# A DiT block on one core: program order made by a list scheduler, x and the FFN weights resident, attention interleaved with the FFN

## The chip, the cores and the metric

The kernel runs on one core of one Trainium2 chip. Time is device time in microseconds (us), from the first to the last instruction of the program. The kernel makes an instruction list for each of five engines, and they run side by side: TensorE (matmuls; PE in the profile, its weight loads PEld), VectorE (DVE), ScalarE (ACT), GpSimd (POOL) and SyncE (SP, which issues the transfers here). The kernel orders them against one another with semaphores.

Every kernel was run several times, and the text gives the median of its runs. Each comparison uses runs of the same chip and the same rounds. A run that is over 1.5 % above the fastest of its kernel counts as slow and is left out of the ratios. A *profiled span* is the span of the one execution that was traced; it is 0.4 to 3.2 us shorter than the median time, and I say which of the two a number is.

## The reference, cut to what matters

```python
# S = 2048 tokens, D = 512, H = 32 heads of 16, F = 1792, everything bf16
mod = (silu(c) @ w_mod)                        # six vectors of 512: sa, ca, ga, sb, cb, gb
h = layernorm(x) * (1 + ca) + sa
q, k, v = h @ wqkv                             # 512 x 1536
# token s sees only the 8 tokens s, s-2, ..., s-14 (window 8, dilation 2)
attn = softmax(q . k[s - 2w] / 4  over w)      # masked where s - 2w < 0
x = x + ga * ((attn . v[s - 2w]) @ wo)
h = layernorm(x) * (1 + cb) + sb
x = x + gb * ((silu(h @ w1) * (h @ w3)) @ w2)  # 512 x 1792, twice, and 1792 x 512
```

Both kernels work on 16 tiles T of 128 tokens and 4 chunks of 512. The attention, with a window of only 8 tokens, makes no matmul of Q with K. Instead VectorE multiplies Q with eight shifted copies of K (the *QK product*, 128x4096 elements), TensorE sums the product over each head with a 0/1 matrix, softmax follows, VectorE multiplies eight shifted copies of V with the weights (the *AV product*), and TensorE sums over the eight shifts with identity matmuls. V goes to DRAM and comes back shifted by a strided load.

Of the kernel before, what the change touches and what calls it, by code (L numbers as in the profile page):

```python
# [1 line left out]

# [8 lines left out]
P = 128  # L11
# [8 lines left out]
NDT = D // P  # L20
NFT = F // P
# [3 lines left out]
XN_SLOTS = 8  # L25
VT_SLOTS = 8
NSL = 6
POOL_BANKS = (0, 1, 4, 5)
OY_BANKS = (2, 3)
L_BANKS = (6, 7)  # L30


class _Sem:
    __slots__ = ("h", "count", "producer")

    def __init__(self, h):
        self.h = h
        self.count = 0
        self.producer = None


class KernelBuilder:
    ENGS = ("sp", "pe", "dve", "act", "pool")

    def __init__(self, nc, ctx: ExitStack):
        self.nc = nc
        self.ctx = ctx
        self.streams = {e: [] for e in self.ENGS}
        self.sems = {}
        self.waited = {}  # L50

    def sem(self, name) -> _Sem:
        s = self.sems.get(name)
        if s is None:
            h = self.ctx.enter_context(self.nc.semaphore(name))
            s = _Sem(h)
            self.sems[name] = s
        return s

    def _inc(self, eng, name, n):  # L60
        s = self.sem(name)
        if s.producer is None:
            s.producer = eng
        assert s.producer == eng, f"sem {name} incremented by {eng} and {s.producer}"
        s.count += n
        return s

    def cur(self, name):
        return self.sem(name).count

    def wait(self, eng, name, value):
        if value is None or value <= 0:
            return
        s = self.sem(name)
        assert value <= s.count, f"wait on {name} for {value} but only {s.count} scheduled (deadlock)"
        key = (eng, name)
        if self.waited.get(key, 0) >= value:
            return
        self.waited[key] = value
        h = s.h  # L80
        self.streams[eng].append(lambda e, h=h, v=value: e.wait_ge(h, v))

    def emit(self, eng, fn, inc=None, incn=1):
        if inc is not None:
            s = self._inc(eng, inc, incn)
            h = s.h
            self.streams[eng].append(lambda e, fn=fn, h=h, n=incn: fn(e).then_inc(h, n))
            return s.count
        self.streams[eng].append(lambda e, fn=fn: fn(e))
        return None  # L90

    def dma(self, eng, out_ap, in_ap, inc):
        s = self._inc(eng, inc, 16)
        h = s.h
        nc = self.nc

        def fn(e, out_ap=out_ap, in_ap=in_ap, h=h):
            with nc.allow_non_contiguous_dma(reason="layout dma"):
                e.dma_start(out_ap, in_ap).then_inc(h, 16)

        self.streams[eng].append(fn)
        return s.count

    def replay(self):
        nc = self.nc
        with nc.Block() as block:
            for eng in self.ENGS:
                fns = self.streams[eng]
                if not fns:
                    continue  # L110
                starter = {"sp": block.sync, "pe": block.tensor, "dve": block.vector,
                           "act": block.scalar, "pool": block.gpsimd}[eng]

                def section(e, fns=fns):
                    for fn in fns:
                        fn(e)

                starter(section)
# [6 lines left out]
def bass_adaLN_cond__sliding_local_dilated__glu_gated_swiglu__prompt_kernel(  # L125
    nc, A_x, A_wqkv, A_wo, B_x, B_w1, B_w3, B_w2, c, w_mod, out, dbg=None
):
    ctx = ExitStack()
    with ctx:
        kb = KernelBuilder(nc, ctx)  # L130
        _build(kb, A_x, A_wqkv, A_wo, B_w1, B_w3, B_w2, c, w_mod, out)
        kb.replay()


def _build(kb: KernelBuilder, A_x, A_wqkv, A_wo, B_w1, B_w3, B_w2, c, w_mod, out):
    nc = kb.nc
    ctx = kb.ctx
    sp, pe, dve, act, pool = "sp", "pe", "dve", "act", "pool"
    bf = dt.bfloat16
    f32 = dt.float32  # L140
# [4 lines left out]
    A_x = _full_ap(A_x)  # L145
    A_wqkv = _full_ap(A_wqkv)
    A_wo = _full_ap(A_wo)
    B_w1 = _full_ap(B_w1)
    B_w3 = _full_ap(B_w3)
    B_w2 = _full_ap(B_w2)  # L150
    c = _full_ap(c)
    w_mod = _full_ap(w_mod)
    out = _full_ap(out)
    x2d = A_x.flatten_outer_dims()
    out2d = out.flatten_outer_dims()
    x_view = x2d.rearrange("(t p) d -> p t d", p=P)

    x_res = [sb([P, D], bf, f"x_res{i}") for i in range(2)]
    x1_tok = sb([P, NT, D], bf, "x1_tok")
    hT = sb([P, NDT, 2, 512], bf, "hT")  # L160
    regW = sb([P, NDT, 3 * D], bf, "regW")
    wqkv_sb = regW
    wo_sb = sb([P, NDT, D], bf, "wo_sb")
    NWS = 6
    w13 = [sb([P, NDT, 2 * P], bf, f"w13_{i}") for i in range(NWS)]
    w2_sb = sb([P, NFT, D], bf, "w2_sb")
    hhb = [sb([P, NFT, 512], bf, f"hh{i}") for i in range(2)]
    hh = hhb[0]
    xn = sb([P, XN_SLOTS, D], bf, "xn")
    stats = [sb([P, NT, 6], f32, f"stats{i}") for i in range(2)]  # L170
    mv = [sb([P, NT, 2], f32, f"mv{i}") for i in range(2)]
    rsn = [sb([P, NT, 2], f32, f"rsn{i}") for i in range(2)]
    cst = sb([P, 4], f32, "cst")
# [3 lines left out]
    ident = sb([P, P], bf, "ident")  # L177
    E_sb = sb([P, NDT, H], bf, "E_sb")
    ones_bf = sb([P, P], bf, "ones_bf")
    cT = sb([P, NDT], bf, "cT")  # L180
    thc = sb([P, NDT], f32, "thc")
    csT = sb([P, NDT], f32, "csT")
    csT_bf = sb([P, NDT], bf, "csT_bf")
# [3 lines left out]
    attn = [sb([P, W, H], bf, f"attn{i}") for i in range(2)]  # L187
    Eexp = [sb([P, W, H], f32, f"Eexp{i}") for i in range(2)]
    oT_sb = [sb([P, NDT, P], bf, f"oT{i}") for i in range(2)]
    o_sb = [sb([P, D], bf, f"osb{i}") for i in range(2)]  # L190
    ga_bc = sb([P, D], bf, "ga_bc")
    gb_bc = sb([P, D], bf, "gb_bc")
    csb = sb([P, NDT, P], bf, "csb")
    junk = [sb([P, D], bf, f"junk{i}") for i in range(2)]

    wbase = nc.lookup_mloc(regW).addr

    def wsb(shape, dtype, name, off):
        return nc.alloc_sbuf_tensor_at("sb_" + name, shape, dtype, offset=wbase + off)

    thb = [wsb([P, 512], bf, f"thb{i}", 3072 * i) for i in range(4)]
    gbf = [wsb([P, 512], bf, f"gbf{i}", 3072 * i + 1024) for i in range(4)]
    ubf = [wsb([P, 512], bf, f"ubf{i}", 3072 * i + 2048) for i in range(4)]

    ARENA = 90112
    arena = sb([P, ARENA], dt.uint8, "arena")
    abase = nc.lookup_mloc(arena).addr

    def asb(shape, dtype, name, off):
        return nc.alloc_sbuf_tensor_at("sb_" + name, shape, dtype, offset=abase + off)  # L210

    qT = asb([P, NDT, S], bf, "qT", 0)
    kT = asb([P, NDT, S], bf, "kT", 16384)
    prodQK = [asb([P, W, NDT, P], bf, f"prodQK{i}", 32768 + 8192 * i) for i in range(2)]
    x_ln = asb([P, NT, D], bf, "x_ln", 73728)
    v_tok = asb([P, VT_SLOTS, D], bf, "v_tok", 49152)
    for i in range(4, NSL):
        thb.append(asb([P, 512], bf, f"thb{i}", 49152 + 3072 * (i - 4)))
        gbf.append(asb([P, 512], bf, f"gbf{i}", 49152 + 3072 * (i - 4) + 1024))
        ubf.append(asb([P, 512], bf, f"ubf{i}", 49152 + 3072 * (i - 4) + 2048))  # L220
    vsh = [asb([P, W, D], bf, f"vsh{i}", 57344 + 8192 * i) for i in range(2)]
    prodAV = [asb([P, W, D], bf, f"prodAV{i}", 73728 + 8192 * i) for i in range(2)]
    wmA = asb([P, NDT, 1536], bf, "wmA", 57344)


    hh_base = nc.lookup_mloc(hh).addr
    wmB = nc.alloc_sbuf_tensor_at("sb_wmB", [P, NDT, 1536], bf, offset=hh_base)

    v_dram = nc.dram_tensor("v_scratch_dram", (S, D), bf)

    PALL = ctx.enter_context(nc.psum_tensor("pall", [P, 8 * 512], f32))

    def bank_f32(b):
        return PALL[:, b * 512:(b + 1) * 512]

    def bank_bf16(b):
        return PALL[:, b * 512:(b + 1) * 512].bitcast(bf)

    pool_state = {"next": 0, "release": {}}

    def pool_acquire():
        i = pool_state["next"]
        pool_state["next"] += 1
        nb = len(POOL_BANKS)
        if i >= nb:
            eng_, semname, val = pool_state["release"][i - nb]
            kb.wait(pe, semname, val)
# [703 lines left out]
```

## The kernel before: what the change and the argument touch

The program order is written by hand. `do_step(s)` starts the QK product of tile s, the softmax of tile s-1, the AV product of s-2, the sums of s-3, the residual of s-4 and LayerNorm 2 behind that:

```python
    def do_step(s, allow_ffn=True):
        if in_range(s - 1):
            L_vals[s - 1] = qk_reduce(s - 1)
            smx_vals[s - 1] = softmax_max(s - 1)
        if in_range(s - 3):
            O_vals[s - 3] = av_acc(s - 3)
        # ... (softmax, QK product of s, AV product of s-2, shifted V load, residual, LN2) ...
                if g == 0:      # after LN2 of chunk 0: ONE VectorE instruction scales all of w2
                    scal["w2"] = kb.emit(dve, lambda e: e.scalar_tensor_tensor(w2_sb[:], w2_sb[:], 0.5, bass.AP(gb_bc, ...),
                                                                              op0=ALU.mult, op1=ALU.mult), inc="dve_p")
                enqueue_ffn_chunk(g)
        if allow_ffn:
            emit_ffn_units(UNITS_PER_STEP, W2_PER_STEP)     # 3.5 FFN units and one w2 product per step
    # ... QKV of all four chunks is issued among do_step(0) ... do_step(10), with allow_ffn=False ...
    do_step(10, allow_ffn=False)
    for s in range(11, nsteps):
        do_step(s)                                          # FFN units only from here
```

No FFN unit can start before QKV of all chunks is done, because the FFN's scratch tiles lie in the memory of `wqkv`. The FFN weights are streamed, each column group once per chunk, so four times:

```python
    def w13_load(n):                                  # n = 14 * chunk + fi
        # ... wait for the slot n % 6 ...
        kb.dma(sp, w13[s_][:, :, 0:P], w1_view[:, :, fi * P:(fi + 1) * P], inc=...)
        w13_dma_val[n] = kb.dma(sp, w13[s_][:, :, P:2 * P], w3_view[:, :, fi * P:(fi + 1) * P], inc=...)
```

ScalarE normalises for LayerNorm, sums for LayerNorm 2 (two passes with an accumulator) and copies both FFN results out of PSUM. x is loaded a second time, tile by tile, for the residual.

## Time and profile before

| Kernel before | |
|---|---|
| time, median of 4 runs | 312.89 us (312.24 to 318.33) |
| profiled span | 311.0 us |
| TensorE's work at full clock | 254 us |
| TensorE's lost time (span less that work) | 57 us |
| first QKV / first QK product / first AV product / first FFN matmul | 21.4 / 31.9 / 53.3 / 120.4 us |
| moved by DMA | 47.2 MB |

The second part of the profile's page gives the busy tenths of each engine in 40 equal slices of 7.8 us; PEclk is TensorE's granted clock in tenths. These are the lines of TensorE, VectorE and the clock, then the engine shares of the chain of work that ended last, of the kernel before:

```profile
PE   0557971899999978399779999989999999999996
DVE  3790655968998999978993999642546435455521
PEclk9999997699999999779979999999999999999999
...
PE 64%; DVE 19%; ACT 6%; POOL 4%; issue 4%; DMA 2%; SPq 0%; DVEq 0%; ACTq 0%
```

TensorE is full from two thirds of the span on, and has holes in the first half. The windows view gives each engine's busy us and instruction count in a stretch, then the granted clock, the DMA engines' busy share and the rate in GB/s. Kernel before:

```profile
core 0: us, PE busy (x) PEld busy (x) DVE busy (x) ACT busy (x) POOL busy (x), PEclk, DMA share, GB/s
0.00:20.00 20.00, 5.47 (x56) 3.34 (x57) 12.53 (x37) 10.33 (x14) 14.66 (x49) 1.00 0.84 289
20.00:40.00 20.00, 17.79 (x125) 9.14 (x125) 10.03 (x29) 16.34 (x27) 9.71 (x33) 1.00 0.60 205
40.00:60.00 20.00, 10.24 (x117) 7.01 (x116) 12.63 (x19) 7.59 (x14) 0.00 (x0) 0.75 0.54 176
...
120.00:140.00 20.00, 14.51 (x109) 7.94 (x108) 17.71 (x19) 11.51 (x26) 12.55 (x11) 0.83 0.54 146
```

Busy time of TensorE overstates its work, since a matmul at half clock is busy for longer (further down, 6 matmuls take 2.60 us at half clock and 10 take 2.32 us at full clock). So I use a ledger in this document: each matmul is charged what it takes at full clock when matmuls run back to back (216 ns with 512 columns and 56 ns with 128, read from the spacing of starts in the trace; 28 ns with 32, from 0.91 us for 32 of them at 34.70 us, where the starts lie 25 ns apart; 25 would make the work 1.5 us less in both kernels), and what is left of the span is *lost*: waits, half clock, start and tail together. The count is the same in both kernels, 936 + 640 + 512 matmuls and 64 tiny ones, 254.3 us.

### The profile page before, as it was taken

How to read it: one execution, taken by the hardware profiler on the slowest of the kernel's cores; microseconds unless marked ns; L12 is line 12 of the kernel's file. 1: busy time of each engine (PE TensorE's matmuls, PEld its weight loads, DVE VectorE, ACT ScalarE, POOL GpSimd, SP SyncE). 2: the span in 40 equal slices, each digit the busy share in tenths (PEclk: the TensorE clock that was granted, in tenths of full speed). 3: DMA queues.
4: the chain of work that ended last, by engine and by line, in shares of the span. 5: the costliest groups of instructions: out<-in, count | busy, mean ns of one | idle time of the engine just before them, and what ended most of it. 6: DMA issues, size and time to landing. Idle time of an engine off the chain costs nothing.

```text
span 311.0 us, 5746 instructions
## 1 busy us (share of the span) xinstructions
PE 265.8 (85%) x2152; PEld 147.4 (47%) x2152; DVE 207.3 (67%) x312; ACT 194.3 (62%) x378; POOL 83.4 (27%) x177
## 2 busy tenths in 40 slices
PE   0557971899999978399779999989999999999996
PEld 0333531666566564166364564554444444444442
DVE  3790655968998999978993999642546435455521
ACT  1588790267565662868749848649776696556600
POOL 6788000002553559735224201101110000000000
PEclk9999997699999999779979999999999999999999
DMA  6989146446446797268564908833336554443001
GB/s 231 376 244 333 67 138 193 153 155 205 168 154 220 214 256 209 52 190 228 129 185 101 235 22 227 179 94 77 86 84 136 120 127 105 104 104 69 19 34 51
DMA packets 87714, 47.24 MB, mean 152 GB/s; under 512 B 60927, under 2 KB 85959, under 8 KB 87687
## 3 DMA queue, kind: packets, MB, share of 16 engines
q1 hardware_dynamic: 86951, 43.47, 50.4%
q0 software_dynamic: 736, 3.41, 3.2%
q8 instruction: 17, 0.28, 0.4%
q14 instruction: 10, 0.08, 0.1%
HBM read 42.67 MB, written 4.19 MB: 151 GB/s over the span
## 4 chain that ended last, share of the span: by engine, by line
PE 64%; DVE 19%; ACT 6%; POOL 4%; issue 4%; DMA 2%; SPq 0%; DVEq 0%; ACTq 0%
PE pall L766 16%; PE pall L716 15%; PE pall L722 14%; PE pall L615 7%; PE pall L456 3%; DVE sb_prodAV_75 L603 3%; DMA sb_wmA<-in_w_mod_dram 2%; DVE sb_prodQK_63 L510 2%; PE pall L430 2%; DVE sb_w_sb L864 2%; DVE sb_prodQK_64 L510 2%; DVE sb_prodAV_76 L603 2%; PE pall L522 2%; PE pall L636 2%; ACT sb_xn L371 2%
## 5 line engine op out<-in xcount | busy, mean ns | idle before, releaser
L766 PE MATMUL pall<-sb_w_sb,sb_hh 128*128 128x512 bf16 x224 | 50.3, 379 | 0.0
L656 POOL TENSOR_TENSOR sb_rsn<-sb_mv 128x1 f32<-128x1 f32 x16 | 9.6, 599 | 136.4 <-ACT sb_junk L653 136.4
L766 PEld LDWEIGHTS pall<-sb_w_sb,sb_hh 128*128 128x128 bf16 x224 | 21.9, 98 | 26.5
L430 PE MATMUL pall<-sb_hT,sb_regW 128*128 128x512 bf16 x128 | 30.2, 390 | 2.9 <-ACT sb_qT L435 2.0
L543 ACT ACTIVATE sb_Eexp<-pall,sb_smx 128x256 f32<-128x256 f32 x16 | 7.6, 476 | 31.4 <-DVE sb_smx L534 31.4
L405 ACT ACTIVATE sb_hT<-pall,sb_modc 128x512 bf16<-128x512 bf16 x32 | 22.3, 777 | 6.2 <-PE pall L390 6.2
L626 ACT ACTIVATE sb_oT<-pall 128x512 bf16<-128x512 f32 x16 | 9.5, 597 | 25.5 <-PE pall L615 25.5
L615 PE MATMUL pall<-sb_ident,sb_prodAV_75 128*128 128x128 bf16 x256 | 17.2, 231 | 8.6 <-DVE sb_prodAV_75 L603 6.6
L775 DVE TENSOR_TENSOR sb_osb<-pall,sb_x_tok 128x512 bf16<-128x512 f32 x16 | 11.1, 691 | 19.7 <-PE pall L766 19.7
L430 PEld LDWEIGHTS pall<-sb_hT,sb_regW 128*128 128x128 bf16 x128 | 12.7, 101 | 18.6 <-ACT sb_qT L435 2.5
L615 PEld LDWEIGHTS pall<-sb_ident,sb_prodAV_75 128*128 128x128 bf16 x256 | 16.0, 104 | 9.2 <-DVE sb_prodAV_75 L603 8.6
L615 PE MATMUL pall<-sb_ident,sb_prodAV_76 128*128 128x128 bf16 x256 | 17.7, 234 | 2.9 <-DVE sb_x_tok L645 2.9
L657 POOL TENSOR_TENSOR sb_rsn<-sb_mv,sb_cst 128x1 f32<-128x1 f32 x16 | 19.7, 1233 | 0.0
L390 PE MATMUL pall<-sb_ident,sb_xn 128*128 128x128 bf16 x128 | 11.4, 242 | 9.6 <-ACT sb_xn L371 9.6
L603 DVE TENSOR_TENSOR sb_prodAV_75<-sb_vsh_73,sb_attn 128x4096 bf16<-128x4096 bf16 x8 | 18.3, 2286 | 0.0
L510 DVE TENSOR_TENSOR sb_prodQK_64<-sb_qT,sb_kT 128x4096 bf16<-128x4096 bf16 x8 | 18.3, 2285 | 0.0
L603 DVE TENSOR_TENSOR sb_prodAV_76<-sb_vsh_74,sb_attn 128x4096 bf16<-128x4096 bf16 x8 | 18.3, 2284 | 0.0
L615 PEld LDWEIGHTS pall<-sb_ident,sb_prodAV_76 128*128 128x128 bf16 x256 | 16.6, 106 | 3.3 <-DVE sb_prodAV_76 L603 2.8
L663 POOL TENSOR_TENSOR sb_rsn<-sb_rsn,sb_cst 128x1 f32<-128x1 f32 x16 | 16.1, 1008 | 1.2
L636 PE MATMUL pall<-sb_wo_sb,sb_oT 128*128 128x512 bf16 x64 | 16.4, 379 | 0.0
L371 ACT ACTIVATE sb_xn<-sb_x_ln,sb_rsn 128x512 bf16<-128x512 bf16 x16 | 12.3, 815 | 6.6 <-POOL sb_rsn L365 6.6
L510 DVE TENSOR_TENSOR sb_prodQK_63<-sb_qT,sb_kT 128x4096 bf16<-128x4096 bf16 x7 | 16.0, 2285 | 0.0
(129 smaller groups left out, 579.9 us busy)
## 6 DMA issues: line engine op xcount, KB each, us to landing
sb_vsh_74<-v_scratch_dram SPq DMA_DIRECT2D x8, 1024.0 KB, 5.5
sb_vsh_73<-v_scratch_dram SPq DMA_DIRECT2D x7, 1024.0 KB
sb_w_0<-in_B_w_dram SPq DMA_DIRECT2D x20, 128.0 KB, 3.0
sb_w_1<-in_B_w_dram SPq DMA_DIRECT2D x20, 128.0 KB, 2.6
sb_w_2<-in_B_w_dram SPq DMA_DIRECT2D x18, 128.0 KB, 2.8
sb_w_3<-in_B_w_dram SPq DMA_DIRECT2D x18, 128.0 KB, 2.6
sb_w_4<-in_B_w_dram SPq DMA_DIRECT2D x18, 128.0 KB, 2.6
sb_w_5<-in_B_w_dram SPq DMA_DIRECT2D x18, 128.0 KB, 2.7
```

Of the source, the lines that this page charges most:

```text
L371: return kb.emit(act, lambda e: e.activation(xn[:, T % XN_SLOTS, :], src_ap, ACT.Identity, bias=rs[:, T, 1:2], scale=rs[:, T, 0:1]), inc=" ...
L405: av = kb.emit(act, lambda e, ft=ft, col=col, trv=trv: e.activation(hT[:, ft, slot, :], trv[:, col:col + 512], ACT.Identity, bias=modc[:, ...
L430: v = kb.emit(pe, lambda e, t=t, bank=bank, wcol=wcol: e.matmul(bank, wqkv_sb[:, t, wcol:wcol + P], hT[:, t, slot, :], start=(t == 0), sto ...
L510: return kb.emit(dve, lambda e, in0=in0, in1=in1: e.tensor_tensor(prodQK[b][:], in0, in1, ALU.mult), inc="dve_qk")
L603: return kb.emit(dve, lambda e: e.tensor_tensor(o_w, v_w, a_w, ALU.mult), inc="dve_av")
L615: v = kb.emit(pe, lambda e, ft=ft, w=w: e.matmul(ob[:, ft * P:(ft + 1) * P], prodAV[b][:, w, ft * P:(ft + 1) * P], ident[:], start=(w == 0 ...
L636: v = kb.emit(pe, lambda e, ft=ft: e.matmul(yb, oT_sb[b][:, ft, :], wo_sb[:, ft, :], start=(ft == 0), stop=(ft == NDT - 1)), inc=("pe_Y" i ...
L657: v = kb.emit(pool, lambda e: e.tensor_tensor(rs[:, T, 1:2], mvb[:, T, 0:1], cst[:, 2:3], ALU.mult), inc="pool_r1")
L663: v = kb.emit(pool, lambda e: e.tensor_tensor(rs[:, T, 0:1], rs[:, T, 0:1], cst[:, 1:2], ALU.pow), inc="pool_r1")
L716: vg = kb.emit(pe, lambda e, t=t, gbank=gbank: e.matmul(gbank, w13[s_][:, t, 0:P], hT[:, t, slot, :], start=(t == 0), stop=(t == NDT - 1)) ...
L722: vu = kb.emit(pe, lambda e, t=t, ubank=ubank: e.matmul(ubank, w13[s_][:, t, P:2 * P], hT[:, t, slot, :], start=(t == 0), stop=(t == NDT - ...
L766: zv = kb.emit(pe, lambda e, fi=fi, zb=zb, hh=hh: e.matmul(zb, hh[:, fi, tt * P:(tt + 1) * P], w2_sb[:, fi, :], start=(fi == 0), stop=(fi ...
```

## The change

Its intent is to keep TensorE fed by running two stages with different limits at the same time: the attention of chunk c+1, which loads VectorE more (about 7 us of its instructions a tile, from 66.39 us in the kernel before, where TensorE's two sums of a tile took 0.91 and 1.79 us and the product with wo 1.03 us), beside the FFN of chunk c, which loads TensorE more. The trace of the kernel before shows both: VectorE busy for 17.71 us and TensorE for 14.51 us from 120 to 140 us, and TensorE alone full at the end (59.97 of the 60 us from 240 to 300 us, VectorE 29.00). The kernel is rewritten around a list scheduler: every instruction is declared with a cost and a priority, a small simulation in the Python of the kernel places them, and each engine runs its resulting order. The instructions are the same kind as before, with these differences:

```diff
+LAT = {"sp": 1900, "pe": 230, "dve": 70, "act": 150, "pool": 120}
+DMA_RATE = 260.0                                  # bytes per ns that the order assumes
+    def schedule(self):
+        # ... at each event: for each free engine take the ready op of lowest priority number
+        #     whose buffers are free; place it at now, busy for o.cost ...
-    for s in range(11, nsteps): do_step(s)             # and in it emit_ffn_units(UNITS_PER_STEP, W2_PER_STEP)
+    def t_attn(T):   return TT * T                                     # priorities
+    def t_ffn(cch, fi):  return TT * (4 * cch + 5.5) + fi * (4 * TT / 20)
-    w13 = [sb([P, NDT, 2 * P], bf, f"w13_{i}") for i in range(NWS)]    # streamed, 4 times
+    w1 = sb([P, KT, F], bf, "w1"); w3 = sb([P, KT, F], bf, "w3")       # resident, loaded once
-    x_ln, x_res (x loaded twice), x1_tok
+    x_sb = sb([P, NT, D], bf, "x")                                     # resident, updated in place
-    LayerNorm: normalise on ScalarE; LN2 sums on ScalarE (2 passes)
+    LayerNorm: bn_stats and normalise on VectorE, both LayerNorms
-    FFN unit: ScalarE tanh, copy of g, copy of u; VectorE g*u, then (tanh+1)*gu
+    FFN unit: ScalarE tanh, copy of u; VectorE (tanh+1)*g read from PSUM, then *u
-    w2 scaled by one scalar_tensor_tensor
+    w2 scaled by two tensor_tensor of half the size
+    p.op("pool", lambda e: e.memset(vpq0.at[:], 0.0), 3600, -7e5, w=[vpq0])    # zero fills, early
+    p.op("pool", lambda e: e.memset(vvsh0.at[:], 0.0), 3600, -7e5, w=[vvsh0])
```

## The prediction

> **What bounds the kernel now.** TensorE, by work and by late feeding. Its work at full clock, from the timeline's spacings: 936 matmuls of 512 columns at 216 ns (fourteen L766 in 3.02 us) = 202 us; 512 AV matmuls (32 in 1.79 us) 29 us; 512 QK matmuls (32 in about 0.9 us) 15 us; transposes 8 us; modulation 2 us: 255 us of a span of 311. The other 56 us are gaps and slow clock. The windows view shows where: gaps until 30 us; 40 to 60 us (PE busy 5.9 and 4.4 of 10, granted clock 0.50 in the second); 110 to 130 us (7.1, 4.5), where one 7.6 us DVE instruction (L864) scales w2; then PE is full from 210 us to the end. FFN starts only at 129 us (first L716), so from 210 us PE works alone while DVE is half idle. The chain of waits: 64% PE, 19% DVE. [...]
>
> **What the change does to each engine** (trace durations):
> - PE: the same 255 us.
> - ACT: loses a second FFN copy (56 x 0.61 = 34 us), the LN normalisation (25 us) and the LN2 sums (20 us plus reads): 194 to about 135 us.
> - DVE: gains LN2 statistics (16 x 0.85 = 14 us) and 32 normalisations (estimate 0.3 us each, since a 128-column tensor_scalar took 0.25: 10 us); the w2 scaling is split and drops from 7.6 to about 4 us: 207 to about 230 us.
> - DMA: w1/w3 are read once, not four times (14.7 to 3.7 MB), x once: 47 to about 34 MB. Loads that wait for nothing, about 13 MB, all queue early on one queue. At 0.32 MB/us (windows 10 to 30 us) they occupy it until about 42 us, so the V write and shifted-V loads behind them land late: first AV product near 47 us (51 before).
>
> **Critical path after.** First QK product near 22 us (32 before). DVE then has four attention tiles (7.1 us each), LN1 ahead and LN2; with the late V, FFN of chunk 0 starts near 72 us instead of 129. By then PE has done about 58 us of work (QKV of three chunks or more, four attention tiles). The remaining 197 us of PE work meets about 175 us of DVE work, so PE is the limit: 72 + 197 + 3 us tail = 272 us if PE never waits. DVE is about 90% loaded in that stretch, both engines run in a fixed order made from a cost model, so I add 5% of the stretch: 282 us.
>
> **Predicted: 282 us, 268 to 299 in 8 of 10. Faster by over 2%: 0.92; within 2%: 0.05; slower: 0.03.**
>
> **What would show it right or wrong.** Right: PE matmul count unchanged, PE full (9 to 10 of 10) from about 75 us to the end with DVE at 8 to 9 of 10; first FFN matmul at 65 to 80 us; ACT near 135 us; DMA near 34 MB; the chain of waits over 70% PE after 75 us. Wrong: FFN matmuls waiting for DVE to free PSUM (g banks are held until a DVE instruction); AV waiting for shifted V after 60 us; PE at half clock beyond 30 us.
>
> **What would make it wrong.** The order's cost model differs from true durations (ACT 540 ns, the trace has 610), so an in-order engine may stall behind a late item; or DVE, not PE, limits the interleaved stretch: then about 290 to 300 us. If the early loads delay V less than I think, 272 us or below.

The marked cut took no term out of the sum, which stands as recorded: 72 + 197 + 3 = 272 us, and 282 us with 5 % of the stretch. The 4 us for the scaling of w2 stand there without a source; an estimate from the kernel before gives the same (7168 columns at the 2.29 us that a QK product of 4096 columns took: 4.0 us), and the kernel after took 3.95 us.

## More of the kernel before

The kernel before loses 17.0 us in its first 20 us, 3.8 in the next 20 and 12.1 from 40 to 60 us.

From 30 us until the clock fell at 50 us, TensorE's pauses were at most 1.9 us.

## The result, and the profile after

The changed kernel takes **297.12 us** (296.91 to 297.40, 4 runs) against 312.89 us: ratio **0.9509**, 95 % interval 0.9487 to 0.953. A ratio here is worked out by the measuring program from the fast runs of both kernels in the same rounds, so it isn't quite the ratio of the medians that I quote. It is faster, by half of what I had forecast.

The same lines of the page and of the windows view, kernel after (slices of 7.4 us):

```profile
PE   0479996699999699999999999699999989999796
DVE  4763988968999969989648997977588851366611
PEclk9999998599999979999999999799999999999999
...
PE 69%; DVE 21%; ACT 4%; issue 2%; POOL 2%; DMA 1%; DVEq 0%
```

```profile
core 0: us, PE busy (x) PEld busy (x) DVE busy (x) ACT busy (x) POOL busy (x), PEclk, DMA share, GB/s
0.00:20.00 20.00, 6.37 (x56) 3.73 (x58) 12.29 (x33) 4.87 (x7) 12.47 (x24) 1.00 0.91 266
20.00:40.00 20.00, 19.48 (x183) 10.46 (x184) 13.72 (x37) 13.94 (x24) 0.00 (x0) 1.00 1.09 350
40.00:60.00 20.00, 14.88 (x151) 8.40 (x152) 18.89 (x25) 8.20 (x15) 1.41 (x3) 0.74 0.49 162
...
120.00:140.00 20.00, 19.84 (x154) 11.63 (x156) 18.55 (x31) 13.46 (x24) 0.88 (x2) 1.00 0.32 105
```

The hole at 120 us is gone. The first 20 us look as before, and from 40 to 60 us TensorE still runs with waits and at a mean clock of 0.74. The ledger, in us:

| | before | forecast | after |
|---|---|---|---|
| profiled span | 311.0 | | 295.4 |
| first FFN matmul | 120.4 | 72 | 103.3 |
| TensorE work done by then | 82.6 | 58 | 74.6 |
| **lost before it** | 37.8 | **14** | **28.7** |
| lost after it | 18.8 | 13 | 12.4 |
| of the loss: 0 to 20 us / 40 to 60 us | 17.0 / 12.1 | | 16.0 / 8.0 |

So the change gained 15.5 us of lost time: 9 before the first FFN matmul and 6 after it. The forecast of the second part held (13 against 12.4). The forecast of the first part was half of what is lost there.

What TensorE waited for in the kernel after, from the waits view (total, times, longest):

```profile
PE pall L460 <- DMA sb_wm_s<-in_w_mod_dram: 9.5, 1, 9.5
PE pall L726 <- DVE sb_hh L715: 5.3, 3, 2.5
PE pall L558 <- ACT sb_h L531: 4.6, 2, 2.7
```

Three places stand out. The *start*: TensorE does nothing until the modulation weights have landed at 9.5 us, and the first QKV matmul runs at 16.47 us. The *chunk ends*: the first w2 product (L726) of a chunk waits up to 2.5 us for the last FFN unit's VectorE work, three times. And the *stretch from 45 to 60 us*, where TensorE waits in small pieces and then runs at half clock. The last shows in windows of 2 us:

```profile
46.00:48.00 2.00, 1.11 (x45) 1.01 (x41) 1.65 (x1) 0.00 (x0) 0.21 (x1) 1.00 1.07 369
48.00:50.00 2.00, 1.30 (x37) 1.30 (x38) 2.00 (x6) 0.00 (x0) 0.00 (x0) 0.76 0.44 149
50.00:52.00 2.00, 0.56 (x6) 0.29 (x3) 2.00 (x1) 1.40 (x2) 0.00 (x0) 0.50 0.00 0
52.00:54.00 2.00, 1.03 (x8) 0.77 (x8) 2.00 (x2) 0.87 (x3) 0.00 (x0) 0.50 0.00 0
...
56.00:58.00 2.00, 2.00 (x6) 0.68 (x5) 2.00 (x2) 1.16 (x3) 0.00 (x0) 0.50 0.56 171
```

What TensorE itself waited for here, by the waits view: 1.59 us for VectorE's QK product (until 48.70 us), then 1.54 and 1.94 us for ScalarE's evacuations of LayerNorm 1 (until 52.10 and 55.07 us). VectorE is full (2.00 of 2.00) and DMA is silent from 50 to 54 us. VectorE's order has two QK products (49.85 us, 4.49 us for both) and the scaling of w2 (54.25 us, 3.95 us) ahead of the first AV product at 61.41 us. Meanwhile the next load of shifted V, issued at 55.98 us, stood behind two V writes in SyncE's order, issued from 55.13 us, which waited for ScalarE copies that began at 54.51 us. That this order of VectorE held TensorE is not shown: from 50 to 55 us it was ScalarE that TensorE waited for. Before the clock fell at 49.0 us TensorE had been idle, since 34 us, only in pieces of at most 1.6 us, and from 46 to 50 us it was busy for 2.41 of 4 us; no run here shows which share of busy time keeps the clock.

Two shorter stretches at half clock follow, 103.7 to 107.1 us, after the first FFN matmuls, and 189.0 to 192.4 us, after the wait at a chunk end.

### The profile page after: what moved, and what is told of

It reads as the page before. It is cut to its first block, busy times and chain, and to the rows that moved or that the text cites. A ratio compares the mean times of both kernels' runs of the same rounds, so it can differ in the third digit from the quotient of the medians.

```text
span 295.4 us, 5127 instructions
## 1 busy us (share of the span) xinstructions
PE 262.3 (89%) x2120; PEld 144.8 (49%) x2152; DVE 216.9 (73%) x369; ACT 134.5 (46%) x228; POOL 32.2 (11%) x60
## 2 busy tenths in 40 slices
DMA packets 34255, 34.10 MB, mean 115 GB/s; under 512 B 1775, under 2 KB 33207, under 8 KB 34231
## 4 chain that ended last, share of the span: by engine, by line
PE 69%; DVE 21%; ACT 4%; issue 2%; POOL 2%; DMA 1%; DVEq 0%
PE pall L702 27%; PE pall L726 17%; PE pall L558 9%; PE pall L674 6%; DVE sb_vsh L665 5%; PE pall L577 4%; DVE sb_pq L618 3%; ACT sb_h L531 3%; DVE sb_th L712 3%; PE pall L686 3%; PE pall L523 2%; PE pall L627 2%; DVE sb_st L493 2%; DVE sb_hh L715 2%; DVE sb_csT L443 1%
## 5 line engine op out<-in xcount | busy, mean ns | idle before, releaser
L702 PE MATMUL pall<-sb_h,sb_w 128*128 128x512 bf16 x435 | 99.7, 383 | 2.5 <-ACT sb_h L531 1.6
L702 PEld LDWEIGHTS pall<-sb_h,sb_w 128*128 128x128 bf16 x448 | 43.6, 99 | 52.9 <-issue 2.3
L726 PE MATMUL pall<-sb_w,sb_hh 128*128 128x512 bf16 x218 | 50.7, 387 | 5.8 <-DVE sb_hh L715 5.3
L712 DVE SCALAR_TENSOR_TENSOR sb_th<-sb_th,pall 128x512 bf16<-128x512 bf16 x56 | 37.8, 683 | 21.7 <-ACT sb_ub L710 21.3
L708 ACT ACTIVATE sb_th<-pall 128x512 bf16<-128x512 f32 x56 | 33.5, 597 | 33.9 <-PE pall L702 33.9
L710 ACT ACTIVATE sb_ub<-pall 128x512 bf16<-128x512 f32 x56 | 33.5, 598 | 28.7 <-PE pall L702 28.7
L726 PEld LDWEIGHTS pall<-sb_w,sb_hh 128*128 128x128 bf16 x224 | 22.1, 100 | 32.8 <-DVE sb_hh L715 6.1
L558 PE MATMUL pall<-sb_h,sb_wqkv 128*128 128x512 bf16 x123 | 32.5, 422 | 5.2 <-ACT sb_h L531 4.6
L665 DVE TENSOR_TENSOR sb_vsh<-sb_vsh,sb_attn 128x4096 bf16<-128x4096 bf16 x16 | 36.5, 2284 | 0.0
L618 DVE TENSOR_TENSOR sb_pq<-sb_q,sb_kT 128x4096 bf16<-128x4096 bf16 x15 | 34.2, 2284 | 1.9 <-PE pall L627 1.9
L674 PE MATMUL pall<-sb_ident,sb_vsh 128*128 128x128 bf16 x512 | 31.2, 219 | 1.0 <-DVE sb_vsh L665 1.0
## 6 DMA issues: line engine op xcount, KB each, us to landing
sb_w<-in_B_w_dram SPq DMA_DIRECT2D x1, 1792.0 KB, 11.5
```

The source lines that it names most:

```text
L558: ins = e.matmul(bank(vp), wqkv[:, t, col:col + P], vh.at[:, t, :], start=(t == 0), stop=(t == KT - 1))
L618: return e.tensor_tensor(vp.at[:], in0, in1, ALU.mult)
L665: return e.tensor_tensor(v_w, v_w, a_w, ALU.mult)
L674: ins = e.matmul(b[:, ft * P:(ft + 1) * P], vv.at[:, w, ft * P:(ft + 1) * P], ident[:], start=(w == 0), stop=(w == W - 1))
L702: ins = e.matmul(bank(vp), wt[:, t, fi * P:(fi + 1) * P], vh.at[:, t, :], start=(t == 0), stop=(t == KT - 1))
L708: p.op("act", lambda e: e.activation(vt.at[0][:], bank(vgp), ACT.Tanh, scale=0.5), 540, pr, r=[vgp], w=[vt])
```

## The experiments

All edits are made to the kernel after, and "order kept" means that the schedule is made as before the edit and then altered at the named place only, so that nothing else moves. The ratio is to the kernel before in the same rounds (its medians there: 312.21, 312.81, 312.31, 312.20 and 312.43 us). Useless filler matmuls are counted as lost time, not as work.

A caution for small differences: the ledger is of one traced run each, and the fast runs of one kernel lie up to 3.1 us apart (e7), in groups that go with their mean granted clock (e7: 289.03 us at 0.994, 290.3 and 290.9 us at 0.988, 292.0 to 292.1 us at 0.981 and 0.982). In the traces of the two kernels the half clock comes in stretches of 3.4, 6.8 or 10.2 us (before: 10.2 from 50.0 us, 6.8 from 128.5 us and 3.4 from 155.8 us; after: 10.2 from 49.0 us and 3.4 from 103.7 and from 189.0 us; the last 0.6 us of the kernel after are a cut piece), and one stretch of 3.4 us more or less is worth up to 1.7 us (an estimate: half of its length). All four runs of the kernel after had a mean clock of 0.97. So I compare runs of equal clock where the record has them.

| run | time, us | ratio | first FFN matmul | lost before it | lost after it |
|---|---|---|---|---|---|
| kernel after | 297.12 | 0.9509 | 103.3 | 28.7 | 12.4 |
| e1_rate330 | 304.09 | 0.9723 | 95.0 | 33.8 | 15.2 |
| e2_v_first | 302.89 | 0.9696 | 91.7 | 30.2 | 15.2 |
| e3_v_first_rate330 | 296.43 | 0.9467 | 86.4 | 28.7 | 11.5 |
| e4_half_av (wrong result) | 291.68 | 0.9329 | 100.6 | 26.0 | 9.0 |
| e5_memset_later | 295.69 | 0.9473 | 101.7 | 27.1 | 12.1 |
| e6_w2_split | 291.30 | 0.9311 | 102.0 | 27.4 | 7.0 |
| e7_warm | 291.47 | 0.9307 | 98.1 | 23.6 | 12.4 |
| e8_all_three | 287.79 | 0.9206 | 100.8 | 26.3 | 6.9 |
| e9_start | 295.52 | 0.9461 | 101.3 | 26.8 | 12.3 |
| e10_best_a | 289.77 | 0.9270 | 88.3 | 31.2 | 2.9 |
| e11_best_b | 294.50 | 0.9432 | 101.7 | 35.9 | 2.2 |
| e12_start_and_three | 285.68 | 0.9124 | 98.7 | 24.2 | 5.3 |
| e13_start_no_filler | 294.03 | 0.9423 | 100.0 | 25.5 | 12.1 |
| e14_all_less_filler | 285.76 | 0.9149 | 98.0 | 23.5 | 7.0 |

### Does an earlier FFN help? e1, e2, e3

My forecast was a sum that began at the first FFN matmul, so the first theory was that the late shifted V delays it, and that bringing V forward brings the time down with it. There are two ways to do that. The order was made for 260 bytes per ns, and the trace shows 350 GB/s from 20 to 40 us; e1 tells the scheduler 330. In e2 the nine loads of FFN weights wait until the four V writes of chunk 0 are out. e3 does both.

```diff
-DMA_RATE = 260.0
+DMA_RATE = 330.0                                   # e1 and e3
         for i in range(4):
             proj_v(4 * cch + i, vh1[cch], base + (20 if cch == 0 else 1200) + i)
+        if cch == 0:                                # e2 and e3
+            for o in w_loads:                       # the loads of w1, w3 and w2
+                o.deps.update({d: True for d in vv_dram[3].writers})
```

> Only the planner's transfer rate is changed, from 260 to the 330 that the windows of 10 to 40 us show, so that the fixed order expects the shifted V when it really comes. Theory A (late start: the order was made for slower transfers, so DVE reaches the first AV product at 61.4 us though its data landed near 50 us, and the FFN starts at 103 us): first AV product before 53 us, first FFN matmul at 85 to 93 us, time 284 to 291 us. Rival B (the work DVE did early is only moved: TensorE's lost time turns up later, at the chunk borders): first FFN matmul at 85 to 93 us as well, but time within 1% of 297 us.

> The nine loads of FFN weights (5.5 MB) wait until the four V tiles of chunk 0 are written; all costs in the planner as they are. Theory C (the V tiles queue behind 13 MB of loads): first AV product near 40 us instead of 61, FFN start near 90 us, time 284 to 290 us. Rival B: FFN start near 90 us, but time within 1% of 297 us, or longer, with TensorE's gaps after 100 us grown by as much as those before it shrank.

> Both changes of the two runs before. Theories A and C together: first AV product near 38 us, FFN start near 80 us, time 280 to 287 us. Rival B: time within 1% of 297 us whatever the start.

All three did what they were meant to do to the attention. The first AV product started at 50.6, 41.2 and 38.8 us instead of 61.4, and the first FFN matmul 8 to 17 us earlier. None is more than half a per cent faster by its ratio than the kernel after, and e1 and e2 are slower by some 2 %. (So e1 fits neither of its ranges, with an FFN start of 95.0 us and a time over 1 % above 297 us. e2 came out as its rival had it, no faster, but not by an exchange: TensorE lost more on both sides of the first FFN matmul, 30.2 and 15.2 us.) TensorE's lost time before the first FFN matmul stayed at 28.7 to 33.8 us: with an earlier FFN less QKV work has been done by then, and it has to be done later. In e1 the loss only moved, into a wait of VectorE for shifted V. Timeline of e1, VectorE (start, duration, what, idle time before it and its releaser):

```profile
64.07 2.29 DVE L665 TENSOR_TENSOR sb_vsh<-sb_vsh,sb_attn 128x4096 bf16<-128x4096 bf16 x1 [6.49 <-DMA sb_vsh<-v_scratch_dram]
```

So the theory that the late V and the late FFN set the time falls. These three runs change the whole order, though, since the scheduler places everything anew; they don't show what one microsecond of V is worth in a fixed order.

### Is VectorE the limit? e4

e4 halves the AV product in a fixed order: VectorE multiplies 4 of the 8 shifts, the rest stays unweighted. Its output is wrong, which doesn't matter for the time. VectorE loses about 1.1 us per tile (1.22 us instead of 2.28).

```diff
-            a_w = bass.AP(ve.at[0], 0, [[W * H, P], [H, W], [0, DH], [1, H]])
-            v_w = bass.AP(vv.at, 0, [[W * D, P], [D, W], [H, DH], [1, H]])
+            a_w = bass.AP(ve.at[0], 0, [[W * H, P], [H, W // 2], [0, DH], [1, H]])
+            v_w = bass.AP(vv.at, 0, [[W * D, P], [D, W // 2], [H, DH], [1, H]])
```

> Wrong result on purpose: the AV product multiplies four of the eight shifts, so each of the 16 takes about 1.15 us instead of 2.28; every engine's order is that of the changed kernel. If DVE's in-order work sets the start of the FFN (61 to 103 us), the first FFN matmul moves from 103 to about 95 us (7 products x 1.13 us) and the time falls by 6 to 10 us, to 287 to 291. If transfers or TensorE set it, the start and the time move by less than 3 us.

VectorE's busy time fell from 217 to 201 us, and the time by 5.4 us, a third of what VectorE was relieved of and less than the 6 to 10 us expected. The first FFN matmul moved only from 103.3 to 100.6 us, as for the case in which transfers or TensorE set it. In its chain of waits nearly nine tenths from 55 us to there is TensorE, the QKV matmuls of later chunks above all, which the order has placed before the FFN; the rest is ScalarE. So from 60 us on the first FFN matmul is late because TensorE has other work to do: in the kernel after, 3.6 of the 43.3 us from 60 us to it are lost. How VectorE holds the rest of the time is less clear. In e4's trace TensorE ran at half clock for 6.8 us between 20 us and the last matmuls, against 17.1 us in the kernel after; half of that difference, 5.1 us (an estimate), is nearly the whole gain.

### The three losses, one by one: e5, e6, e7, and together: e8

The lost time has places, so each was taken away in the kept order.

e5, the start. In the kernel after, a zero fill of GpSimd runs beside three short VectorE instructions. Timeline of the kernel after:

```profile
5.33 3.69 DVE L443 CAST sb_csT<-sb_csT_bf 128x4 f32<-128x4 bf16 x1
5.46 3.56 DVE L493 BATCH_NORM_STATS2 sb_st<-sb_x 128x6 f32<-128x512 bf16 x2
5.49 3.51 POOL L398 MEMSET sb_vsh<- 128x4096 bf16 x1
```

A cast of four elements per partition took 3.69 us; in the kernel before it took 0.17. e5 moves the two fills behind the LayerNorm 1 work of GpSimd.

```diff
+    _move(p, p.named["ms_pq"], p.named["rstd", 0, 3])     # after LN1 of chunk 0 on GpSimd
+    _move(p, p.named["ms_vsh"], p.named["rstd", 0, 4])    # after LN1 of chunk 1 on GpSimd
```

> Every engine's order stays that of the changed kernel, but for the two 3.5 us memsets on GpSimd: they are moved behind the LN1 scale factors of chunk 0 and of chunk 1. Theory S (start: GpSimd is busy with the two memsets until 9 us, which delays LN1 and slows DVE's small instructions; TensorE loses 16 us there): the first QKV matmul moves from 16.5 to 13.5 to 14.5 us and the time falls by 2 to 3 us, to about 294.5 us. Rival W (the start waits for the modulation weights, which land at 9.5 us): first QKV matmul stays within 0.7 us and the time within 1 us of 297.1.

The cast took 0.17 us, so the fill had made it slow. But the start was not earlier: the first QKV matmul ran at 16.85 us. The fills had been moved onto other VectorE instructions:

```profile
8.78 3.51 POOL L418 MEMSET sb_pq<- 128x4096 bf16 x1
...
10.99 1.43 DVE L530 TENSOR_SCALAR sb_xn<-sb_x,sb_mv,sb_rs 128x512 bf16<-128x512 bf16 x1
...
20.09 3.51 POOL L419 MEMSET sb_vsh<- 128x4096 bf16 x1
...
20.18 4.20 DVE L530 TENSOR_SCALAR sb_xn<-sb_x,sb_mv,sb_rs 128x512 bf16<-128x512 bf16 x3 [1.41 <-POOL sb_rs L523]
```

A normalisation takes 0.41 us alone; here one took 1.43 us, and three took 4.20. The slow instructions ended within 0.15 us of the fill beside them: in the kernel after the slow cast ended at 9.02 us and the fill beside it at 9.00 (by the profile the cast had even started first), in e5 the slow normalisation ended at 12.42 and its fill at 12.29, while the fill itself took 3.51 us in every case. A cast that read PSUM while e5's first fill ran, at 10.91 us, took 0.17 us as ever. Why an instruction is held so, the traces do not show.

So e5 was a poor test of the start, and it stays for e9. Nor is its 1.4 us a gain of the edit as far as the record shows. The first 20 us lose 16.0 us as before. Four runs of e5 had a mean clock of 0.975 to 0.977 and took 295.3 to 295.7 us; the two at 0.970 took 297.0 and 297.4 us, no less than the kernel after at that clock (296.9 to 297.4 us). Whether the edit or chance gave the higher clock is open.

e6, the chunk ends. The first w2 product of each chunk is 14 matmuls that wait for all 14 FFN units. e6 cuts it after 10, so that only the last 4 wait.

```diff
-        p.op("pe", mm, NF * MM, pr, r=[vhh[(cch, fi)] for fi in range(NF)] + [vw2s], w=[vz])
+        # order kept; matmuls 0..9 wait for units 0..9, matmuls 10..13 follow as their own item
+        _split(p, first[0], first[1], CUT, first[2])      # CUT = 10
```

> Orders unchanged; the first w2 product of each chunk is cut after 10 of its 14 matmuls, and the first part no longer waits for the last four hidden tiles. Theory T (chunk ends: three waits of a w2 product for the last hidden tile cost TensorE 5.3 us): those waits shrink below 1 us in sum and the time falls by 3.5 to 5 us, to 292 to 293.5. If that wait were hidden elsewhere, the time stays within 1 us.

The ratio went from 0.9509 to 0.9311, and the lost time after the first FFN matmul from 12.4 to 7.0 us. The wait of 2.49 us at 188.81 us in the kernel after became 0.34 us:

```profile
188.81 2.60 PE L726 MATMUL pall<-sb_w,sb_hh 128*128 128x512 bf16 x6 [2.49 <-DVE sb_hh L715]
```

```profile
184.84 2.32 PE L763 MATMUL pall<-sb_w,sb_hh 128*128 128x512 bf16 x10
187.50 1.04 PE L763 MATMUL pall<-sb_w,sb_hh 128*128 128x512 bf16 x4 [0.34 <-DVE sb_hh L752]
```

The first fence is the kernel after, the second e6. The theory that the chunk ends cost their waits holds, but not they alone: the gain of 5.8 us is more than the 3.5 to 5 expected. The wait at 188.81 us had been followed by half clock, and in e6 that stretch is gone too (windows of the kernel after, then of e6; the clock is the third figure from the end):

```profile
189.00:192.40 3.40, 3.18 (x8) 1.22 (x8) 3.40 (x4) 0.47 (x1) 0.16 (x1) 0.50 0.00 0
```

```profile
184.00:188.00 4.00, 3.66 (x46) 1.95 (x45) 4.00 (x9) 0.34 (x1) 1.01 (x2) 1.00 0.54 189
```

On the other side 1.6 us came back as waits of transposes for VectorE's normalisations (3.4 us in e6, 1.8 in the kernel after). No run parts the waits from the clock.

e7, the clock. 190 useless matmuls of the identity with itself (128 columns, 10.7 us at full clock by the ledger's 56 ns) fill TensorE's idle time: 60 before the modulation, 18 and 36 up to the first QKV matmul, 24 and twice 26 between 44 and 51 us. They write PSUM that nobody reads.

```diff
+    _warm(p, 60, None, low)                     # before the first matmul
+    _warm(p, 18, p.named["mod", 0], low)        # after the modulation matmuls
+    _warm(p, 36, last, low)                     # after the transposes of chunk 0
+    _warm(p, 24, p.named["red", 3][0], high)    # 44 to 51 us, between waits
+    for h in range(2):
+        _warm(p, 26, max((p.named["tr", 0, 2, h, t] for t in range(4)), key=...), high)
```

> Orders unchanged; 190 useless matmuls of 128 columns are put into TensorE's idle stretches before 16 us and between 47 and 55 us. Theory K (slow clock after idling: the first 31 QKV matmuls from 16.5 us took 9.7 us and the 31 from 55 us 8.9 us, against 6.7 at full clock): both groups take about 6.7 us, granted clock in the window 50 to 60 us rises from 0.54 to over 0.9, and the time falls by 3 to 5 us, to 292 to 294. If DVE's order holds that stretch and not TensorE, the clock rises and the time stays within 1 us of 297.1.

The ratio went to 0.9307. The first 32 QKV matmuls took 7.08 us, and so did the 32 from 51 us on, where the kernel after needed 8.83 us for 30 and 8.94 us for 31. (In its first group the starts lie 0.43 us apart until 21.57 us and 0.22 us from 21.86 us on, while the windows view prints a clock of 1.00; that this was half clock is inferred from the spacing.) The clock from 50 to 60 us, kernel after and then e7:

```profile
50.00:60.00 10.00, 6.52 (x28) 3.03 (x27) 9.69 (x9) 6.30 (x11) 0.20 (x1) 0.54 0.29 94
```

```profile
50.00:60.00 10.00, 9.91 (x91) 5.45 (x89) 8.60 (x10) 7.68 (x14) 1.21 (x2) 1.00 0.59 195
```

The theory that the half clock costs about as much as its slow matmuls show holds: 5.6 us of time (3 to 5 expected) for 10.7 us of useless matmuls. The half clock after the first FFN matmul stayed, from 98.4 to 101.8 us in e7's trace.

e8 makes the three edits together.

> The three edits together, other orders unchanged. If the lost time of TensorE is a sum of separate losses, the gains add up: 8.5 to 13 us, a time of 284 to 288.5 us. If a loss that is removed turns up again further on, the sum is under 6 us.

287.79 us, 9.3 below the kernel after, where the three gains sum to 12.8 (1.4 + 5.8 + 5.6), of which the 1.4 are doubtful. They overlap or hinder one another. One hindrance shows in the trace: the zero fill that e5 had moved to 20.50 us made a normalisation of chunk 1 take 3.57 us, and TensorE lost 2.5 us from 20 to 40 us, where e7 lost 0.1. In that stretch its clock was 0.50 from 32.4 to 35.7 us. The trace is of e8's slowest run.

### The start once more: e9, e13, and on top of the three: e12, e14

e9 takes the first fill away almost wholly (only the corners that are read are zeroed), sets the second behind the normalisations of chunk 0, and puts VectorE's modulation casts after them.

```diff
-    p.op("pool", lambda e: e.memset(vpq0.at[:], 0.0), 3600, -7e5, w=[vpq0])
+    for w in range(1, W): e.memset(vpq0.at[:, w, :, 0:2 * w], 0.0)    # seven small fills
+    # order kept, but: VectorE's 4 modulation casts of chunk 0 after its 4 normalisations;
+    # the fill of vsh waits for the 4th normalisation
```

> The changed kernel with its order kept, and only the start altered: the zero fill of the first product buffer writes just the corners that are read (seven small memsets on GpSimd in place of one of 3.5 us), the zero fill of the first shifted-V buffer comes after the four norms of chunk 0, and VectorE takes the four modulation casts of chunk 0 after the norms instead of before. Theory S (the late first QKV matmul is made by those two memsets and by that order, and most of the start's loss with it): the first QKV matmul moves from 16.5 us to 14 to 14.8 us and the time falls by 1.5 to 3 us, to 294 to 296 us. Rival (the load of the modulation weights, landed at 9.9 us, and the transposes and evacuations behind it set the start): first QKV matmul at 15.8 us or later and the time changes by less than 0.7 us.

The time is in the theory's range (295.52 us), but the intervals of e9 and the kernel after overlap (0.9429 to 0.9493 and 0.9487 to 0.953), and the two runs of e9 at a clock of 0.970 took 296.8 and 296.9 us. The place doesn't fit: the first QKV matmul ran at 16.00 us. The second fill now ran beside two of the casts:

```profile
9.32 3.51 POOL L430 MEMSET sb_vsh<- 128x4096 bf16 x1 [0.51 <-DVE sb_xn L541]
...
10.72 2.13 DVE L499 CAST sb_modc<-sb_modc_bf 128x4 f32<-128x4 bf16 x1
10.80 2.06 DVE L501 TENSOR_SCALAR sb_onep_bf<-sb_modc_bf 128x4 bf16<-128x4 bf16 x1
```

e13 is e9 with that fill behind the last cast.

> The changed kernel's order with only the start altered, as in e9, but the zero fill of the first shifted-V buffer waits for the last modulation cast of chunk 0, and no filler matmuls. In e9 the two casts beside that fill took 2.1 us each and ScalarE's first evacuation waited for them until 13.16 us. Theory S3 (these slow casts were all that held the start in e9): casts 0.17 us each, the first evacuation at 11.2 to 12.2 us, the first QKV matmul at 14.0 to 15.0 us, and 292.5 to 294.8 us, 1 to 3 us below e9's 295.5. Rival (the first 20 us are not worth what they lose, because TensorE, started earlier, waits for the next group instead): the first QKV matmul moves so, but the time stays within 0.7 us of 295.5.

The casts took 0.17 us each. The first evacuation started at 12.38 us and the first QKV matmul at 15.22 us, both 0.2 us later than the ranges I gave:

```profile
11.07 0.17 DVE L500 CAST sb_modc<-sb_modc_bf 128x4 f32<-128x4 bf16 x1
...
12.38 2.79 ACT L564 ACTIVATE sb_h<-pall,sb_modc 128x512 bf16<-128x512 bf16 x4 [8.38 <-PE pall L556]
15.22 0.61 PE L591 MATMUL pall<-sb_h,sb_wqkv 128*128 128x512 bf16 x1 [2.67 <-ACT sb_h L564]
```

The time is 294.03 us, 1.5 below e9 (ratio 0.9423 against 0.9461; the intervals, 0.9394 to 0.9453 and 0.9429 to 0.9493, overlap). At equal clock the difference stays: at 0.970 e13 took 295.5 and 295.8 us and e9 296.8 and 296.9 us; at 0.975 to 0.977 e13 took 293.2 to 294.1 us and e9 294.5 to 295.9 us. The direction is the theory's and these are few runs, so I call it supported, not shown. Loss in the first 20 us fell from 16.0 to 14.5 us. What remains is a chain: modulation weights at 9.84 us, transposes at 10.69 us behind the modulation matmuls in TensorE's order, four evacuations of 2.79 us. No order tried here got below 14 us of loss in the first 20 us without filler.

e12 is e8 with this start.

> The three edits of e8 together with the start of e9 mended: the zero fill of the first shifted-V buffer now waits until VectorE has done the last modulation cast of chunk 0, because in e9 it ran beside two of these casts and made them 2.1 us each instead of 0.17. Theory S2 (the late first QKV matmul is made by zero fills beside VectorE's short instructions): first QKV matmul at 14 to 14.7 us, the casts 0.2 us each, and the time 284.5 to 286.5 us, 1.5 to 3 us below the 287.8 of the three edits. Rival (the start is not made by that): first QKV matmul at 15.8 us or later, or the start earlier and the time within 0.8 us of 287.8, because the gain is given back in a later wait.

285.68 us: with e14 the best time, 4.0 % below the kernel after by the ratios (0.9124 over 0.9509, each to the kernel before in its own rounds). The gain over e8 came, but not where I said: the first QKV matmul stayed at 16.88 us, because the 18 filler matmuls took 1.96 us (109 ns each; the mean clock from 10 to 14 us was 0.57) and held the transposes until 12.08 us. The gain over e8 stands at equal clock too, 1.8 us on the mean both at 0.994 (286.9 to 287.0 us in e8, 284.2 to 285.9 us in e12) and at 0.988. In the two traces it is in the stretches after the start, but e8's trace is of a run at 0.982 and e12's of one at 0.994, so part of what they differ by is clock. No fill runs beside the normalisations of chunk 1 any more; one of them takes 0.41 us instead of 3.57, and the loss from 20 to 40 us fell from 2.5 to 0.1 us. From 100 to 120 us it fell from 2.2 to 0.0; e8's trace has half clock from 100.6 to 103.9 us there, e12's has none.

e14 leaves these 18 out.

```diff
-    _warm(p, 18, p.named["mod", 0], low)
```

> As e12_start_and_three, less the 18 filler matmuls between the modulation matmuls and the transposes. In e12 the first QKV matmul stayed at 16.88 us: the fillers ran at about 109 ns each and held the transposes from 10.3 until 12.1 us. Theory S3: transposes at 10.4 us, the first QKV matmul at 14.5 to 15.3 us, and a time 1 to 2 us below e12's 285.7, 283.5 to 284.9. Rival (without these fillers the clock falls back for the first QKV group, or the gain is lost in a later wait): time within 0.7 us of 285.7 or above.

The transposes started at 10.57 us as expected, and the time did not move (285.76 us): the rival holds. The other 36 fillers, now at half clock (0.50 from 10 to 14 us), took 4.05 us where e12's took 2.23, and held the first QKV matmul until 16.47 us. Filler is no free gift: its length has to be chosen for the clock it runs at, 2.23 or 4.05 us for the same 36 here.

### Does a freely made order do better? e10, e11

These two apply the lessons to the source and let the scheduler place everything anew. e10 assumes 330 bytes per ns, holds the FFN weights back, normalises on ScalarE, limits how far QK products run ahead, fills the planned gaps and cuts the w2 product. e11 assumes 360, does not hold the weights back and allows four tiles ahead.

```diff
-DMA_RATE = 260.0
+DMA_RATE = 330.0                                           # e11: 360.0
-        vn = ... p.op("dve", tensor_scalar(... subtract, mult))
+        vn = ... p.op("act", activation(Identity, bias=-mean*rstd, scale=rstd))
-            p.op("dve", prod, 2290, pr, r=[vq[cch]] + ks, w=[vp])
+            p.op("dve", prod, 2290, pr, ..., after=[av_ops[T - 2]] if T >= 2 else [])   # e11: T - 4
+    _fill(p)      # fillers in the gaps that the order has before the FFN is under way
+    # and the small zero fills, the w2 cut (CUT = 10); e10 also holds w1, w3, w2 back as e2
```

> The experiments' lessons in one freely ordered kernel: the list scheduler told 330 bytes per ns of DMA, the FFN weights held back until the V writes of chunk 0, LayerNorm's norms on ScalarE, the QK product of a tile not before the AV product two tiles earlier, small zero fills, the first w2 product of each chunk cut after 10 of 14, and filler matmuls in the planned idle gaps of TensorE. If TensorE's loss (startup, cold clock, chunk ends) is what stands between the changed kernel and its 255 us of work, this has to reach 278 to 285 us, with at most 25 us lost and the first FFN matmul near 76 to 85 us; if the losses move elsewhere (VectorE or ScalarE late once the order is tight), it stays at 287 us or above, no better than the three edits together (287.8).

> As e10_best_a, but with 360 bytes per ns, the FFN weights not held back, and the QK product not before the AV product four tiles earlier: it shows whether the gain hangs on one lucky order. Expected 278 to 286 us and within 2 % of e10_best_a if the removed losses are what counts; more than 2 % apart if the order is what counts.

Both missed their ranges: 289.77 and 294.50 us, worse than the three edits in the old order. That is what I had set down as the sign that the losses move elsewhere. The part after the first FFN matmul is all but clean, 2.9 and 2.2 us lost. The losses are before it. From the waits of VectorE in e10, and of TensorE:

```profile
DVE sb_vsh L746 <- DMA sb_vsh<-v_scratch_dram: 8.6, 1, 8.6
```

```profile
PE pall L755 <- DVE sb_vsh L746: 6.9, 1, 6.9
```

With DMA assumed faster, the order put an AV product where its shifted V had not landed; VectorE stood 8.6 us, and TensorE 6.9 us behind it. It is the same wait as in e1, where the assumed rate was the only edit; that the rate made it here too is inferred. The two are 1.7 % apart, within the 2 % that I had set, but two orders don't show how far luck goes.

## Why the prediction was right or wrong

**Right: the direction, the limit, and the second half.** TensorE's work was unchanged (254.3 us in both traces, forecast 255), ScalarE's busy time was 134.5 us (135), DMA moved 34.10 MB (34) and was full until some 43 us (42; a busy share of 1.10 from 41 to 42 us, 0.82 in the next and 0.23 from 43 to 44 us). After the first FFN matmul 12.4 us were lost (13: 5 % of the stretch and the tail). VectorE's busy time was 216.9 us, not 230; I did not follow that up, as it isn't a term of the sum.

**The term that failed** is this step: "with the late V, FFN of chunk 0 starts near 72 us instead of 129. By then PE has done about 58 us of work". Together these two say that TensorE loses 14 us before its first FFN matmul. It lost 28.7, at 103.3 us with 74.6 us of work done. The miss of 15.1 us, from 282 to 297.1, is made up so: 14.7 more lost before the FFN, 0.6 less lost after it, 0.7 less work than the 255 forecast, and 1.7 by which the median time exceeds the profiled span, which I had not separated. The mechanism (the hole at 110 to 130 us goes, TensorE stays the limit) was right, though no run parts the interleaving from the halved scaling of w2 or the other parts of the rewrite; the size of this term was half of the truth. The "129" in it is a misreading that the sum does not use: the first L716 of the kernel before runs at 120.4 us.

**Why it was too small.** The trace of before shows a loss of 17.0 us in the first 20 us alone, more than I charged for 72. I had read "gaps until 30 us" and then estimated the new start as if residency and reordering mended it. The change leaves the startup chain as it is: modulation weights, modulation matmuls, casts, evacuation, first QKV matmul; it even put zero fills beside its VectorE instructions. The measured loss is 16.0 us. The other large piece is 8.0 us from 40 to 60 us, waits and half clock. I named "PE at half clock beyond 30 us" as a sign of being wrong, and it came: 0.50 from 50 to 58 us, and twice for 3.4 us later.

**A wrong lever.** I wrote the sum as starting time plus remaining work, which makes the first FFN matmul look like the thing to move. e1, e2 and e3 moved it 8 to 17 us forward and gained nothing beyond half a per cent: the loss before it stayed at 28.7 to 33.8 us, and the work not done by then came later. What counts is the time TensorE loses, wherever it is. Taking losses away directly did pay: the half clock 5.6 us (e7), the chunk ends with the half clock behind one of them 5.8 us (e6), both and the start 11.4 us (e12). e12 and e14 reach 285.7 us, which lies 4 us above the forecast of 282.

**What of my warnings came true.** An engine in a fixed order standing behind a late item did, in e1 and e10. In the kernel after, VectorE at 49.85 to 58 us had QK products and the scaling of w2 before AV work, but it was busy, not stalled, and no run prices that order. FFN matmuls waiting for VectorE to free PSUM did not come: their one wait for another engine was 1.6 us, for ScalarE. V later than 60 us did not hold VectorE in the kernel after; it did in e1 and e10, where the order counted on it.

**Open.** The change is one rewrite, and no run takes a single part of it back, so what interleaving, resident weights and the work moved off ScalarE gave each is not shown. Between 23 and 26 us are still lost before the FFN in the best versions, of which filler is 10; how much of the start a different chain (modulation weights split, transposes before the modulation matmuls) would save was not tried. And e1 to e3, e10 and e11 each changed the whole order, so no single wait in them is priced by itself.

## What to carry to other kernels

Before forecasting a reordering, write a ledger of the lost time of the limiting engine by stretch, and for each stretch say which edit removes it; what no edit touches (here the start) stays in the sum. The start of a stage is not a lever by itself: in e1 to e3, moving it forward without removing idle time only exchanged work. Small, local edits in a kept order (cut an accumulation where it waits, keep the clock up, move a fill away from short instructions) added 11.4 us to the 15.8 of the rewrite, while newly made orders, with the same lessons in their source, lost part of it in a wait for data that came later than the order had assumed. Before a gain of 1 or 2 us is put down to an edit, compare runs of equal granted clock: e5's 1.4 us did not outlast that.
